# Feed-forward keys and gates for 512 tokens at once: wider matmuls behind a local-global attention kernel

## The chip, the cores and the metric

One core of one Trainium2 chip runs the whole program. The metric is device time in microseconds, the median of three runs: 692.88 us before the change (692.82 to 693.06).

## The reference, cut to what matters

```
for each of 8 batches, 8 heads of 64:          # attention
    global queries (32) attend to all 544 keys
    local queries (512) attend to 32 global keys and to local keys at most 32 away
x = heads side by side                          # 8 x (32 + 512) tokens x 512
xk = mu_k * x + (1 - mu_k) * x_prev             # token before, the first one sees zeros
xr = mu_r * x + (1 - mu_r) * x_prev
k = relu(xk @ w_k)                              # 512 -> 1024
out = sigmoid(xr @ w_r) * (k * k @ w_v)         # 1024 -> 512, gate of 512
```

All of it is asked for in float32. The weights arrive as float64 words.

## The kernel before

Everything is transposed: features lie on the 128 partitions and tokens along the free dimension, so a product for the feed-forward part is `weights (128x128, loaded into the array) x tokens (128x256, streamed)`. Each float32 operand is split into a high and a low part of the type fp32r, and a product is three matmuls: high by high, high by low, low by high (`products`, L506, the three at L508, L509 and L510).

For a batch there are two halves of 256 tokens (`Tokens`). For each half `mix` (L524) makes xk and xr as high and low parts (difference and weighted sum on DVE, high part by a cast on ACT, low part by a subtraction on POOL, L544). `squares` (L571) makes the keys: 8 blocks of 128 features, two to a PSUM bank, each of 4 x 3 matmuls; ACT takes the relu, DVE multiplies with the product. `gates` (L585) makes 4 blocks of the gate in the same way, with a tanh on ACT.

From batch 2 on (`FROM = 2`) the values `k*k @ w_v` go by seven products of half size instead of eight (`Keys`, L620). The four blocks B11, B12, B21, B22 of the squared keys (first or second half of the features, first or second half of the tokens) are combined to four others, T1 to T4 (`differences`, on DVE). Each block is split into high and low (`split`: cast on ACT, subtraction on DVE for B blocks and on POOL for T blocks), and multiplied with a combination of the value weights that is read back from DRAM (`load_left`, tiles `a`, five buffers, each product needs two). `values_1` makes three products of 24 matmuls each, `values_2` makes four; their results are added on DVE and ACT and multiplied with the gate in `write`, on POOL where the result lies in SBUF.

The attention of batch b+1 (`attention`, in pairs of units: scores, softmax on DVE, ACT and POOL, transposes on the PE, then `weighted`, the products with V) is recorded step by step between the steps of the feed-forward part of batch b (`beside_heads`). Its last result, `xT`, is what the next `mix` reads. The order in which the instructions really stand on each engine is set by a scheduler that works on this recording with its own idea of when an instruction becomes ready; `tc.high_priority()` moves an instruction ahead in it. Each engine then works strictly in that order. All DMAs stand in one queue, SP's.

In a batch of the steady state the PE's order is: `values_1` of the batch before, keys and gates of the first half, `values_2`, keys and gates of the second half, with the attention of the next batch in between. PSUM has three banks for the feed-forward part, four for scores and one for transposes.

## Time and profile before

| | us |
|---|---|
| median of 3 runs | 692.88 |
| lowest, highest | 692.82, 693.06 |
| span of the profiled execution, first to last instruction | 689.8 |
| between span and median | 3.1 |
| PE busy in the span | 663.3 (96%) |
| DVE, ACT, POOL busy | 425.9, 387.5, 359.4 |
| mean granted TensorE clock | 0.992 |

The profile is one execution on the same core, and 3.1 us of the time lie around its span. "Busy" of the PE counts a matmul from its start to a modelled end, some 280 ns for one of 128x256, though the next starts after a little over 110 ns; so what a matmul costs is read from the starts in the timeline or from the chain, not from the mean duration. Each matmul has a weight load of its own, shown as the engine PEld. Matmuls of plain float32 (attention) stand twice in the trace, since each is carried out in two passes.

### The profile page before, as it was taken

How to read it: one execution, taken by the hardware profiler on the slowest of the kernel's cores; microseconds unless marked ns; L12 is line 12 of the kernel's file. 1: busy time of each engine (PE TensorE's matmuls, PEld its weight loads, DVE VectorE, ACT ScalarE, POOL GpSimd, SP SyncE). 2: the span in 40 equal slices, each digit the busy share in tenths (PEclk: the TensorE clock that was granted, in tenths of full speed). 3: DMA queues.
4: the chain of work that ended last, by engine and by line, in shares of the span. 5: the costliest groups of instructions: out<-in, count | busy, mean ns of one | idle time of the engine just before them, and what ended most of it. 6: DMA issues, size and time to landing. Idle time of an engine off the chain costs nothing.

```text
span 689.8 us, 18729 instructions
## 1 busy us (share of the span) xinstructions
PE 663.3 (96%) x7530; PEld 626.6 (91%) x7530; DVE 425.9 (62%) x1221; ACT 387.5 (56%) x1058; POOL 359.4 (52%) x363
## 2 busy tenths in 40 slices
PE   6979999999998999999999999999999999999997
PEld 3769789989897999999999989999999999999997
DVE  5795977457557566545675657645575656377531
ACT  5876866366355565757457563747466644443530
POOL 5577595147777344565338244655348332642810
PEclk9989999999999999999999999999999999999999
DMA  8734353154737740544818092735727090535666
GB/s 343 299 122 169 124 196 127 48 185 141 254 131 253 248 157 29 210 159 151 310 67 302 12 358 92 263 105 204 256 97 271 2 334 34 200 119 172 207 197 208
DMA packets 43542, 123.37 MB, mean 179 GB/s; under 512 B 4032, under 2 KB 20928, under 8 KB 43456
## 3 DMA queue, kind: packets, MB, share of 16 engines
q1 hardware_dynamic: 43456, 122.18, 50.0%
q8 instruction: 59, 0.97, 0.5%
q14 instruction: 27, 0.22, 0.1%
HBM read 104.86 MB, written 17.30 MB: 177 GB/s over the span
## 4 chain that ended last, share of the span: by engine, by line
PE 67%; DVE 12%; POOL 7%; DMA 6%; issue 3%; ACT 3%; SPq 0%; POOLq 0%; ACTq 0%; DVEq 0%
PE ps_m L670 16%; PE ps_m L508 11%; PE ps_m L509 11%; PE ps_m L510 11%; PE ps_s L365 9%; DMA a<-scratch 4%; PE ps_t L394 3%; DVE xfull L539 2%; DVE Pt L333 2%; PE ps_t L361 2%; DVE diff L535 2%; PE ps_s L367 2%; DMA w<-w_k 1%; DVE B L651 1%; POOL Pt L349 1%
## 5 line engine op out<-in xcount | busy, mean ns | idle before, releaser
L508 PE MATMUL ps_m<-xkh,wk_h 128*128 128x256 f32 x544 | 154.3, 285 | 3.3 <-DVE xfull L539 3.3
L509 PE MATMUL ps_m<-xkl,wk_h 128*128 128x256 f32 x544 | 153.2, 282 | 1.0 <-POOL xkl L544 1.0
L510 PE MATMUL ps_m<-xkh,wk_l 128*128 128x256 f32 x544 | 152.5, 281 | 0.0
L670 PE MATMUL ps_m<-bh,a 128*128 128x256 f32 x736 | 137.5, 282 | 3.2 <-DMA a<-scratch 3.1
L339 ACT ACTIVATE Pt<-Pt,m 128x160 f32<-128x160 f32 x256 | 106.5, 419 | 26.7 <-DVE m L333 26.7
L670 PEld LDWEIGHTS ps_m<-bh,a 128*128 128x128 f32 x736 | 114.9, 188 | 6.1 <-DMA a<-scratch 3.7
L349 POOL TENSOR_TENSOR Pt<-Pt,ssum 128x512 f32<-128x512 f32 x64 | 67.4, 1053 | 80.7 <-DVE ssum L295 32.4
L508 PEld LDWEIGHTS ps_m<-xkh,wk_h 128*128 128x128 f32 x544 | 103.0, 190 | 4.9 <-ACT xkh L543 3.8
L509 PEld LDWEIGHTS ps_m<-xkl,wk_h 128*128 128x128 f32 x544 | 102.8, 189 | 2.5 <-POOL xkl L544 1.7
L510 PEld LDWEIGHTS ps_m<-xkh,wk_l 128*128 128x128 f32 x544 | 102.8, 189 | 0.0
L670 PE MATMUL ps_m<-bl,a 128*128 128x256 f32 x368 | 102.5, 279 | 0.0
L544 POOL TENSOR_TENSOR xkl<-xfull,xkh 128x512 fp32r<-128x512 f32 x34 | 46.8, 1375 | 85.9 <-ACT xkh L543 80.9
L582 DVE TENSOR_TENSOR B<-ps_m,relu 128x512 f32<-128x512 f32 x52 | 35.9, 690 | 72.1 <-ACT relu L580 72.0
L580 ACT ACTIVATE relu<-ps_m 128x512 f32<-128x512 f32 x52 | 31.0, 597 | 82.9 <-PE ps_m L510 80.7
L508 PE MATMUL ps_m<-xrh,wr_h 128*128 128x256 f32 x272 | 77.3, 284 | 0.0
L509 PE MATMUL ps_m<-xrl,wr_h 128*128 128x256 f32 x272 | 76.2, 280 | 0.0
L510 PE MATMUL ps_m<-xrh,wr_l 128*128 128x256 f32 x272 | 76.0, 279 | 0.0
L333 DVE CUSTOM_DVE_ANT_0 Pt<-ps_s,masks 128x160 f32<-128x160 f32 x256 | 65.9, 317 | 6.6 <-PE ps_s L365 4.9
L670 PEld LDWEIGHTS ps_m<-bl,a 128*128 128x128 f32 x368 | 69.2, 188 | 0.0
L617 POOL TENSOR_TENSOR gate<-sum,gate 128x512 f32<-128x512 f32 x18 | 26.8, 1489 | 59.7 <-DVE sum L716 39.9
L205 ACT CAST bh<-B 128x512 fp32r<-128x512 f32 x76 | 45.9, 620 | 18.0 <-PE ps_m L670 11.6
L508 PEld LDWEIGHTS ps_m<-xrh,wr_h 128*128 128x128 f32 x272 | 51.5, 189 | 1.2 <-ACT kkh L564 0.6
(146 smaller groups left out, 1594.6 us busy)
## 6 DMA issues: line engine op xcount, KB each, us to landing
a<-scratch SPq DMA_DIRECT2D x92, 512.0 KB, 5.9
raw_qk<-qk SPq DMA_DIRECT2D x32, 768.0 KB, 5.6
raw_v<-v SPq DMA_DIRECT2D x32, 640.0 KB, 6.0
out_l<-gate SPq DMA_DIRECT2D x32, 256.0 KB, 4.6
w<-w_k SPq DMA_DIRECT2D x8, 512.0 KB, 9.7
w<-w_v SPq DMA_DIRECT2D x8, 512.0 KB, 3.9
w<-w_r SPq DMA_DIRECT2D x4, 512.0 KB, 3.5
scratch<-wv_h SPq DMA_DIRECT2D x8, 256.0 KB, 2.8
```

Of the source, the lines that this page charges most:

```text
L205: nc.scalar.copy(hi, val)
L333: read = nc.vector.tensor_tensor_reduce(out=Pt[:, i], in0=place(e, t, h), in1=masks[:, e, slots[t][1]], op0=ALU.add, op1=ALU.min, scale=-s ...
L339: nc.scalar.activation(Pt[:, i], Pt[:, i], AF.Exp, bias=low_x[:, i:i + 1], scale=-1.0, accum_out=ssum[:, i:i + 1],)
L349: nc.gpsimd.tensor_mul(out, Pt[:, each, at:at + n], rinv.unsqueeze(2).to_broadcast([P, 4, n]))
L365: self.last = nc.tensor.matmul(*a, **kw)
L508: nc.tensor.matmul(out, w_h[:, i, cols], x_h(i), start=(i == 0), stop=False)
L509: nc.tensor.matmul(out, w_h[:, i, cols], x_l(i), start=False, stop=False)
L510: nc.tensor.matmul(out, w_l[:, i, cols], x_h(i), start=False, stop=(i == n - 1))
L544: nc.gpsimd.tensor_sub(lo[:, both], xf, hi[:, both].bitcast(F32))
L580: nc.scalar.activation(rk, kp, AF.Relu)
L582: nc.vector.tensor_mul(k2[f0 // HC][f0 % HC // 2], kp, rk)
L670: nc.tensor.matmul(out[:, j], w, x[:, i % 2], start=fresh and (i, j, n) == (0, 0, 0), stop=(i, n) == (HC - 1, 2), skip_group_check=True,)
```

## The change

From batch 2 on the keys and gates of a batch are made for all 512 tokens at once: a matmul streams 128x512 instead of 128x256, and there are half as many of them. A key block now fills a PSUM bank by itself. Only the first two batches and the global tokens stay at 256.

- `Batch.mix` makes xk or xr of 512 tokens, one feature block of 128 at a time. The two are made at different times now, since both use the same four buffers: xk before `values_1`, xr after the keys and before `values_2`.
- The order of a batch is now `values_1` of the batch before, all keys, `values_2`, all gates (`wide`). The first such batch (`first_wide`) has the gates ahead of the keys, and its xk in a pool of its own.
- The squared keys lie in tiles that hold both token halves, so that the blocks of the half-size products are strided parts of them (2 runs of 256). The number of half-size products, their matmuls (128x256), their weights and loads stay as they are. The split of T2 moves from the end of the batch into `values_1`, those of T3, T1, T4, B22 and of the next B11 and B21 follow one product each.
- The pools of the early part (`stage`, `mlp1`, `mlp`) are closed after batch 1, and new ones take their place (`ktp` 7 buffers, `partp` 5, as before `leftp` 5 and `sump` 3).
- The transposes of the attention get a priority of 400 in the scheduler, in all batches (`AHEAD`).

Two places show what that does to the order. First the PE, at the step from `values_1` to the keys in a batch of the steady state, before (`bh` and `bl` are the high and low parts of the blocks; `Pgl` and `Pt` belong to the attention):

```order
L394 MATMUL ps_t<-ident,Pt 128x128 x4
L367 MATMUL ps_s<-raw_qk 64x160
L365 MATMUL ps_s<-raw_qk 64x160 x15
L670 MATMUL ps_m<-bh,a 128x256
L670 MATMUL ps_m<-bl,a 128x256
L670 MATMUL ps_m<-bh,a 128x256 x2
L403 MATMUL ps_t<-ident,Pgl 128x128 x2
...
L508 MATMUL ps_m<-xkh,wk_h 128x256
L509 MATMUL ps_m<-xkl,wk_h 128x256
L510 MATMUL ps_m<-xkh,wk_l 128x256
```

and now, where the rows begin with the products with V (`PT`, `PG`, `PTg`) that make the last `xT` of the next batch:

```order
L371 MATMUL ps_s<-PG,raw_v 64x32 x20
L371 MATMUL ps_s<-PT,raw_v 64x64 x16
L371 MATMUL ps_s<-PTg,raw_v 128x2x64 x8
L401 MATMUL ps_t<-ident,Pt 128x128 x4
L659 MATMUL ps_m<-bl,a 128x256
...
L411 MATMUL ps_t<-ident,Pgl 128x128 x2
...
L373 MATMUL ps_s<-raw_qk 64x160
L371 MATMUL ps_s<-raw_qk 64x160 x15
L401 MATMUL ps_t<-ident,Pt 128x128 x4
L517 MATMUL ps_m<-xkh,wk_h 128x512
L518 MATMUL ps_m<-xkl,wk_h 128x512
L519 MATMUL ps_m<-xkh,wk_l 128x512
```

The matmuls of the keys are twice as wide. Between the products with V and the first key stood 69 of the 72 matmuls of `values_1` and 16 score matmuls; now it is 32 of them (27, two transposes, then 5), 16 score matmuls and 10 transposes.

Second POOL, in the same stretch. `xkl` is the low part of xk that the keys read; `gate<-sum` is the first result of `values_1` times the gate. Before, with `xkl` in halves of 128x512 for two feature blocks of 256 tokens:

```order
L544 TENSOR_TENSOR xkl_5397<-xfull_5403,xkh_5396 128x512 [waits PE_49,Activation_49,Pool_49]
...
L544 TENSOR_TENSOR xkl_5397<-xfull_5416,xkh_5396 128x512 [waits Activation_49]
L544 TENSOR_TENSOR xrl_5399<-xfull_5421,xrh_5398 128x512 [waits Activation_49]
L206 TENSOR_TENSOR bl_5577<-B12_5031,bh_5576 128x512 [waits PE_49,Activation_49]
L206 TENSOR_TENSOR bl_5581<-B12_5032,bh_5580 128x512 [waits Activation_49,Pool_49]
L206 TENSOR_TENSOR bl_5585<-B11_4449,bh_5584 128x512 [waits Activation_49]
L617 TENSOR_TENSOR gate_4591<-sum_5456,gate_4591 128x512 [waits DMAHW3_49,DMAHW5_49,DMAHW2_49,DVE_49]
```

and now, one `xkl` for each of four feature blocks of 512 tokens:

```order
L694 TENSOR_TENSOR xkl_6100<-xfull_6102,xkh_6099 128x512 [waits PE_49,Activation_49,Pool_49]
L694 TENSOR_TENSOR xkl_6100<-xfull_6108,xkh_6099 128x512 [waits Activation_49]
...
L212 TENSOR_TENSOR bl_6248<-kt_5300,bh_6247 128x512 [waits Activation_49]
L608 TENSOR_TENSOR gate_5982<-sum_6157,gate_5982 128x2x256 [waits DMAHW0_49,DMAHW1_49,DVE_49,Pool_49]
L212 TENSOR_TENSOR bl_6252<-kt_5351,bh_6251 128x512 [waits Activation_49]
L694 TENSOR_TENSOR xkl_6114<-xfull_6116,xkh_6113 128x512 [waits Activation_49]
L212 TENSOR_TENSOR bl_6684<-kt_5394,bh_6683 128x512 [waits PE_49,Activation_49]
L694 TENSOR_TENSOR xkl_6114<-xfull_6122,xkh_6113 128x512 [waits Activation_49]
```

The last two `xkl` stood ahead of the gate and of the splits of `values_2`; now they stand behind the gate and two splits.

The diff, cut to its core:

```diff
@@ transposes, transposes_of_g, transposes_global (the same in all three)
-            nc.tensor.transpose(tp[:, i], r.Pt[:, 4 * e + i, SG * e:SG * e + W], ident)
+            with tc.high_priority(AHEAD):
+                nc.tensor.transpose(tp[:, i], r.Pt[:, 4 * e + i, SG * e:SG * e + W], ident)
@@ class Batch(Values), new
+        def mix(self, of, pool=None):
+            mu = mu_k_sb if of == "k" else mu_r_sb
+            hs, ls = self.x[of] = [], []
+            for c in range(NC):
+                if c % 2 == 0:
+                    for part, x in ((hs, "h"), (ls, "l")):
+                        part.append((pool or mixp).tile([P, 2, SL], F32R, tag="mix", name=f"x{of}{x}"))
+                hi, lo = (part[c // 2][:, c % 2] for part in (hs, ls))
+                xT = xT_of(self.b, c)
+                diff, xf = (tmpp.tile([P, SL], F32, tag="tmp", name=name) for name in ("diff", "xfull"))
+                nc.vector.tensor_sub(diff, xT[:, 1:SL + 1], xT[:, 0:SL])
+                nc.vector.scalar_tensor_tensor(xf, diff, mu[:, c:c + 1], xT[:, 0:SL], op0=ALU.mult, op1=ALU.add)
+                nc.scalar.copy(hi, xf)
+                nc.gpsimd.tensor_sub(lo, xf, hi.bitcast(F32))
+        def keys(self):
+            for f in range(NF):
+                a, i = divmod(f, HC)
+                kt = self.blocks(a) if i % 2 == 0 else kt
+                kp = psum("m")
+                products(kp, wk_h, wk_l, slice(f * P, (f + 1) * P), *self.inputs("k"), NC)
+                square(kp, kt[:, i % 2].rearrange("p t n -> p (t n)"), lambda x: x)
+                yield
...
         def values_1(self):
...
+            self.split("T2")
             yield
...
-            t.write(0, c11)
+            self.write(0, 0, c11)
+            self.split("T3")
             yield
...
-            yield
-            self.split("T3", "T1", "T4")
+            self.split("T1")
+            yield
@@ the last level
+    def wide(this, before):
+        this.mix("k")
+        yield from before.values_1()
+        yield from this.keys()
+        this.mix("r")
+        yield from before.values_2(this.split)
+        this.differences()
+        yield from this.gates()
...
+    for b in range(FROM, B):
+        this = Batch(b)
+        steps = wide(this, last) if b > FROM else first_wide(this, last)
+        if b < B - 1:
+            beside_heads(steps, 19 if b > FROM else 16)
```

More of the change, by code (lines that the diff above doesn't have):

```diff
@@ L49 @@
 HUGE = 3.0e38
+AHEAD = 400
 REBIAS = 2.0 ** -112
@@ L705, in values_2 @@
             nc.scalar.copy(u3, X)
-            self.split("B22")
+            self.split("T4")
             yield
@@ L984, in local_global_attention_then_rwkv_ffn, with narrow_batch, first_wide @@
-    final = Keys([global_tokens()])
-    t, = final.tokens
-    for _ in batch(B - 1, last):
-        pass
-    last = keys_of[B - 1]
+    leftp = sump = ktp = partp = None
+    def narrow_batch(b, before):
+        sums = sums_of_values() if b == FROM - 1 else iter(())
+        for n, _ in enumerate(feed_forward(tokens_of(b), before)):
+            if n > FF_STEPS and n % 2:
+                next(sums, None)
+            yield
+        for _ in sums:
+            pass
+    def first_wide(this, before):
+        nonlocal leftp, sump, ktp, partp
+        this.mix("r")
+        yield from before.values()
+        valueu.close()
+        narrow.close()
+        ktp, leftp, sump = (place(*x) for x in (("ktp", 7), ("leftp", 5), ("sump", 3)))
+        mixed = ExitStack()
+        this.mix("k", mixed.enter_context(
+            tc.tile_pool(name="mixed", bufs=4, side="right", reuse_waits="tile")
+        ))
+        load_left()
+        load_left()
+        yield from this.gates()
+        yield from this.keys()
+        mixed.close()
+        partp = place("partp", 5)
+        this.split("B11", "B21")
+        this.differences()
@@ new lines, in wide, with place @@
+    def wide(this, before):
+        this.mix("k")
+        yield from before.values_1()
+        yield from this.keys()
+        this.mix("r")
+        yield from before.values_2(this.split)
+        this.differences()
+        yield from this.gates()
+    def place(name, bufs):
+        return last_pools.enter_context(tc.tile_pool(name=name, bufs=bufs, side="right", reuse_waits="tile"))
+    last_pools = ExitStack()
+    last = None
+    for b in range(1, FROM):
+        beside_heads(narrow_batch(b, last), 2 * FF_STEPS + 4)
+        last = feed_forward.last
@@ L990, in end @@
+    change_use(MIDDLE_USE)
+    for b in range(FROM, B):
[3 more added lines that the diff above has]
+            beside_heads(steps, 19 if b > FROM else 16)
+        else:
+            for _ in steps:
+                pass
+        last = this
+    t = global_tokens()
+    final = Globals(t)
     def end():
```

205 lines of the change are left out of this document (94 added, 111 removed).

## Prediction

> **What bounds the kernel now.** I read the engines' busy shares first, then the PE's waits, then the stretches of single batches, then the chain of waits.
>
> ```profile
> PE 663.3 (96%) x7530; PEld 626.6 (91%) x7530; DVE 425.9 (62%) x1221; ACT 387.5 (56%) x1058; POOL 359.4 (52%) x363
> PE ps_s L361 <- DMA raw_qk<-qk: 5.5, 2, 4.9
> PE ps_m L508 <- DVE xfull L539: 3.3, 1, 3.3
> PE ps_m L670 <- DMA a<-scratch: 3.1, 3, 1.5
> 270.00:347.00 77.00, 76.78 (x909) 73.35 (x908) 45.58 (x147) 44.79 (x128) 38.57 (x37) 1.00 0.50 186
> 347.00:424.00 77.00, 75.56 (x902) 72.47 (x901) 47.73 (x146) 44.70 (x127) 38.22 (x37) 1.00 0.51 186
> 501.00:578.00 77.00, 76.90 (x897) 74.36 (x896) 48.92 (x132) 43.27 (x115) 35.72 (x34) 1.00 0.46 165
> PE 67%; DVE 12%; POOL 7%; DMA 6%; issue 3%; ACT 3%; SPq 0%; POOLq 0%; ACTq 0%; DVEq 0%
> ```
>
> The PE is busy 96% of the span. The first two waits, for the first inputs and for the first mix, lie in the start that the change hardly touches. A batch of the steady state takes 77 us, and in the windows of 77 us the PE is busy for 75.6 to 76.9 of them (the number behind the window's length), at full granted clock (1.00). What idles there is mostly the wait for the value weights `a`, 3.1 us in all. So the bound is the pace at which the PE takes its matmuls, and a change pays only through fewer or cheaper ones. The 12% of DVE in the chain is no reserve: it followed releases back, while the PE had other work.
>
> **The wide matmuls.** From batch 2 on there are 6 batches, each with (32 + 16) blocks x 4 x 3 / 4 = 144 matmuls of 128x512 in place of 288 of 128x256: 8 key blocks and 4 gate blocks x 12, and twice that before. In all 864 pairs become one each. Their present price, from the chain and from starts in the PE's timeline:
>
> ```profile
> 611.33 5.44 PE ps_m L670 x48
> 413.31 0.28 PE L508 MATMUL ps_m<-xkh,wk_h 128*128 128x256 f32 x1
> 416.02 0.28 PE L510 MATMUL ps_m<-xkh,wk_l 128*128 128x256 f32 x1
> ```
>
> 48 matmuls in 5.44 us are 113.3 ns each. From 413.31 to 416.02 lie 23 steps of 2.71 us, 117.8 ns each: there are two paces, and in the stretches I looked at neither prevails. I take the middle, 115.5 ns, so 231 ns for a pair.
>
> What would one of 512 cost? No row of before shows one. What sets the pace of the narrow ones is seen in the attention:
>
> ```profile
> 434.73 0.22 PE L367 MATMUL ps_s<-PT,raw_v 128*64 128x64 f32 x1
> 435.66 1.31 PE L365 MATMUL ps_s<-PG,raw_v 128*64 128x32 f32 x40
> 436.80 1.13 PE L365 MATMUL ps_s<-PT,raw_v 128*64 128x64 f32 x32
> 419.55 0.60 PE L394 MATMUL ps_t<-ident,Pt 128*128 128x128 f32 x4
> L394 PE MATMUL ps_t<-ident,Pt 128*128 128x128 f32 x256 | 38.5, 275 | 2.8 <-POOL Pt L349 2.0 <-ACT xT L500 0.6 <-ACT PT L396 0.2
> L365 PE MATMUL ps_s<-raw_qk 128*64 128x384 f32 x36 | 7.6, 501 | 0.0
> L365 PE MATMUL ps_s<-raw_qk 128*64 128x32 f32 x36 | 2.3, 208 | 0.0
> ```
>
> With the last one's own 0.22 us taken off, the 40 of 32 columns start (1.31 - 0.22) / 39 = 28 ns apart and the 32 of 64 columns (1.13 - 0.22) / 31 = 29 ns: twice the columns, the same pace, with the same 64 columns of weights. The transposes load 128 columns of weights and stream 128: (0.60 - 0.275) / 3 = 108 ns. The matmul with 256 columns, with as large a load, takes 113. So up to here it is the load of the weights that sets the pace, and columns come nearly free. Long streams do cost: 384 columns against 32 cost 501 - 208 = 293 ns more, 0.83 ns for a column of plain float32. The fp32r ones stream 256 in at most 113 ns, 0.44 each, so they run at about double rate, 0.416; 512 columns are 213 ns, and some 3 ns for the change of matmul make 216, with the load hidden under the stream. A pair saves 231 - 216 = 15 ns, and 864 of them 13.0 us. That is the value I take. Bounds: no better per column than the fast pace, 226.6 ns, saves 3.8 us; the slow pace in all, 235.6 ns, costs 4.0 us; 213 ns saves 15.6 us.
>
> The Trainium skill (TensorE: Matmul & The Clock Gate, section "Back-to-back issue gap") gives N / 2.4 + 2.5 ns for a warm matmul; that would be 215.8 ns here, and the term 13.1 us. The same page (section "What overlaps and what doesn't" of the part on packing) says that a weight load overlaps a running matmul only where the row group differs, which would speak against hiding the load, since all these use the whole array; the pace of 113 ns for a load and a stream together speaks for overlap. It is a rival below.
>
> **Waits for `a`.** Two of the three lie in `values_2`, where the tile took long to land:
>
> ```profile
> 394.86 0.81 SPq L282 DMA_DIRECT2D raw_qk<-qk  x2
> 398.56 0.80 SPq L287 DMA_DIRECT2D raw_v<-v  x2
> 399.66 9.09 DMA a<-scratch
> 476.44 9.20 DMA a<-scratch
> a<-scratch SPq DMA_DIRECT2D x92, 512.0 KB, 5.9
> ```
>
> The median is 5.9 us; these two stood behind loads of qk and V issued just ahead (two of each, from 394.86 on, for the first). In the new order the products with V come at the very start of `values_2`, so V is loaded earlier and the later products of that stretch have 3 us or more of other work before a sixth tile is needed. I take 2.0 us as saved, of bounds 3.1 and -3 (as many waits again).
>
> **The mix of xk.** This is the step that gets worse. The mix for 512 tokens needs the last `xT`, and the queues of DVE and POOL hold other things between. Durations:
>
> ```profile
> L544 POOL TENSOR_TENSOR xkl<-xfull,xkh 128x512 fp32r<-128x512 f32 x34 | 46.8, 1375 | 85.9 <-ACT xkh L543 80.9 <-issue 5.0
> L206 POOL TENSOR_TENSOR bl<-B,bh 128x512 fp32r<-128x512 f32 x36 | 47.0, 1322 | 2.2 <-ACT bh L205 2.2
> L617 POOL TENSOR_TENSOR gate<-sum,gate 128x512 f32<-128x512 f32 x18 | 26.8, 1489 | 59.7 <-DVE sum L716 39.9 <-DVE sum L709 19.8
> L691 DVE TENSOR_TENSOR sum<-ps_m,sum 128x512 f32<-128x512 f32 x6 | 4.1, 686 | 4.7 <-PE ps_m L670 2.9 <-PE ps_t L394 1.8
> 437.86 1.16 PE L365 MATMUL ps_s<-PTg,raw_v 64*128 64x128 f32 x16
> 443.73 1.29 POOL L544 TENSOR_TENSOR xkl<-xfull,xkh 128x512 fp32r<-128x512 f32 x1 [1.02 <-ACT xkh L543]
> 449.51 0.28 PE L508 MATMUL ps_m<-xkh,wk_h 128*128 128x256 f32 x1
> 445.32 1.12 PE L365 MATMUL ps_s<-raw_qk 64*64 64x160 f32 x27
> ```
>
> Before, the products with V end at 439.0, the last `xkl` is done at 445.0, and the first key starts at 449.5: 4.5 us of slack. Now, with the end of the products with V as zero: the second product of `values_1` has 8 matmuls left, after four transposes, so it ends at about 0.6 + 0.9 + 0.2 = 1.7; DVE's sum 0.69; then POOL has the gate, a split, the third `xkl`, a split, the fourth `xkl`: 1.49 + 1.32 + 1.375 + 1.32 + 1.375 = 6.9. The fourth is there at 9.3. The PE has until then four transposes (0.6), 27 and 5 matmuls (3.6), two transposes (0.25), 16 scores (1.25) and four transposes (0.6), 6.3 us, and reads the fourth low part in the 11th matmul of the first key, 2.2 us later: at 8.5. So the PE waits about 0.7 us, where POOL runs at 1.3 us each 0.3 us; I take 0.5 in batches 3 to 6, 2 us. In the last batch there is no other attention: 36 matmuls of `values_1` follow the products with V (4.1 us), and the key needs the low part at about 6.1, while POOL's row is done at 9.1: 3 us. Together 5 us lost. Bounds: 0, where the operations overlap better, and 15 us, where POOL's share is 2 us longer in each of the five.
>
> xr has it easier: between the end of the keys and the gates lie at least 60 matmuls and the products with V, over 10 us for four `xkl`-like steps of 1.4. Its DVE work grows by the second difference only (as many elements as the first), with DVE at 62%.
>
> **The rest.** In the first wide batch the split of B11 waits for the keys' buffers, and only scores and two transposes lie ahead of its product: 1 us lost, bounds 0 and 3. The store of the gate in halves, the strided blocks and the splits in their new places cost the same instructions on engines at 52 to 62%; they are hidden behind the PE's 77 us, and where POOL's cover is gone it is counted above. The transposes ahead in the schedule are the same transposes; they change the first 255 us by chance, where the PE idles some 14 us, and I take 0, bounds 2 either way.
>
> **Sum**, against the profiled execution's own span: 689.8 - 13.0 - 2.0 + 5.0 + 1.0 = 680.8, and the 3.1 us between span and median give 683.9. I take the timed executions to have the same 3.1 us around a span. **Forecast: 684 us.**
>
> **Rivals.**
> 1. The wide matmul gains nothing per column over the fast pace (226.6 ns). For it: no fp32r of more than 256 columns is in the trace, and the rate of 0.416 is taken from plain float32. Against: the pace did not depend on columns where the load is the same. Time: 692.9 - 3.8 - 2.0 + 6.0 = 693.1, no change.
> 2. Slower: POOL's row in front of the fourth `xkl` becomes the new bound of a batch. One mechanism: where the normalisation of a scores unit stands there too, it adds 2 x (1.05 + 0.46) = 3.0 us:
>
> ```profile
> L349 POOL TENSOR_TENSOR Pt<-Pt,ssum 128x512 f32<-128x512 f32 x64 | 67.4, 1053 | 80.7 <-DVE ssum L295 32.4 <-ACT xrh L543 23.2 <-PE ps_s L365 10.7
> L349 POOL TENSOR_TENSOR Pgl<-Pt,ssum 128x128 f32<-128x128 f32 x64 | 29.7, 463 | 0.0
> ```
>
>    Then 5 x 3.0 more: 699 us. It decides once the waits exceed 14 us over five batches, 2.8 us each. Against it: in the order as it stands those normalisations come behind the fourth `xkl`, and POOL is half idle.
> 3. Better than the sum: POOL's row keeps pace, the waits for `a` go, and the start loses a little idle time: 692.9 - 13.0 - 3.1 + 1.0 = 677.8, with 1 us of the start 677.
> 4. The load is not hidden under a matmul of the same rows: 213 + 108 = 321 ns each, with the transposes' pace as the load's price, which by 864 x (321 - 231) is 78 us more: 692.9 + 78 - 2.0 + 6.0 = 775 us. The row of 113 ns for stream and load speaks against it. It is the rule of overlap of the Trainium skill (TensorE: Matmul & The Clock Gate) named above.
>
> That the change would not do what it says is excluded for the wide matmuls: the order shows them, 864 of them.
>
> **How the numbers follow.** Chances: the forecast's case 0.60 (679 to 689), rival 1 0.13, rival 2 0.10, rival 3 0.15, rival 4 0.02. About 0.2% (1.4 us) is what a measurement of this kernel can tell from no change. Faster: 0.60 + 0.15 and a third of rival 1, 0.79. Within 0.2%: a third of rival 1 and part of rival 2, 0.07. Slower: 0.14. The range, 677 to 691, takes in the forecast's case, most of rival 3 and the better side of rival 1, and leaves 0.2 out.
>
> **What would show it.** Starts of the wide matmuls 216 ns apart in the chain, and 864 of them: 227 or more would make rival 1 right. Waits of the PE on `xkl` of 0.5 us in a steady batch and 3 us in the last one; a batch of 77 us shortened to about 75. No wait for `a` over 1 us in `values_2`. The forecast is wrong if the PE idles over 10 us behind batch 2, or if the batch stays at 77 us while it does not idle.

## The result, and the profile after

The changed kernel takes 740.66 us (median of 4 runs, 738.59 to 741.18) against 692.85 us before (691.66 to 693.06, 4 runs on the same chip): a ratio of 1.069, with a 95% interval from 1.067 to 1.072. The forecast was 684 us, with a range up to 691. The profiled execution has a span of 738.6 us, 48.8 more than before.

The stages below are cut, in both traces, at the first half-size matmul of each `values_1`; the keys and gates of the first wide batch lie ahead of the first cut.

| stage | before, us | after, us | more |
|---|---|---|---|
| up to the first half-size product | 280.1 | 294.9 | 14.8 |
| batch stage 1 | 76.1 | 86.2 | 10.1 |
| batch stage 2 | 76.8 | 83.5 | 6.7 |
| batch stage 3 | 76.9 | 82.2 | 5.3 |
| batch stage 4 | 72.3 | 75.2 | 2.9 |
| batch stage 5 (attention runs out) | 56.2 | 63.5 | 7.3 |
| global tokens, and the end | 51.5 | 53.1 | 1.6 |

No stage became shorter. Busy shares, chain and the PE's waits after (in us: total, times, longest):

```profile
PE 688.3 (93%) x6666; PEld 598.6 (81%) x6666; DVE 463.4 (63%) x1173; ACT 387.9 (53%) x1058; POOL 380.5 (52%) x363
...
PE 51%; DVE 19%; POOL 12%; issue 7%; ACT 6%; DMA 4%; POOLq 0%; SPq 0%; DVEq 0%; ACTq 0%
PE ps_t L401 <- ACT PTg L412: 4.8, 3, 2.2
PE ps_m L659 <- ACT sum L756: 4.5, 3, 1.9
PE ps_t L411 <- DVE PT L403: 3.6, 4, 1.6
PE ps_t L401 <- POOL xrl L694: 3.1, 1, 3.1
PE ps_m L659 <- DMA a<-scratch: 0.7, 1, 0.7
```

The PE has 864 matmuls fewer and is busy 25 us longer. It now waits in many places for ACT, DVE and POOL, none of which is busy more than 63%. The windows of batch stages 1 to 3 show two things more (length of the stretch, then busy time of PE, PEld, DVE, ACT and POOL, then the granted clock):

```profile
294.90:381.10 86.20, 82.03 (x759) 68.38 (x759) 68.33 (x153) 46.32 (x132) 47.62 (x39) 0.96 0.50 166
381.10:464.60 83.50, 79.87 (x757) 68.58 (x755) 53.69 (x137) 46.93 (x132) 43.61 (x41) 0.96 0.50 171
464.60:546.80 82.20, 78.58 (x757) 67.30 (x755) 53.67 (x137) 44.25 (x126) 40.62 (x36) 0.98 0.51 174
```

DVE has 54 to 68 us of work in these stages, where it had 45 to 49 before, and the clock is no longer 1.00. One stall, from the timelines of PE, DVE and ACT in batch stage 2, shows how both come about:

```profile
434.49 1.60 DVE L692 SCALAR_TENSOR_TENSOR xfull<-diff,mu_k_sb,xT 128x512 f32<-128x512 f32 x1
436.20 1.60 DVE L691 TENSOR_TENSOR diff<-xT 128x512 f32<-128x512 f32 x1
437.71 0.69 DVE L755 TENSOR_TENSOR ps_m<-ps_m,sum 128x512 f32<-128x512 f32 x1
438.44 0.59 ACT L756 COPY sum<-ps_m 128x512 f32<-128x512 f32 x1 [3.55 <-DVE ps_m L755]
439.07 0.39 PE L659 MATMUL ps_m<-bh,a 128*128 128x256 f32 x1 [1.92 <-ACT sum L756]
439.30 0.28 PE L659 MATMUL ps_m<-bl,a 128*128 128x256 f32 x1
440.91 1.08 PE L401 MATMUL ps_t<-ident,Pt 128*128 128x128 f32 x4 [1.34 <-ACT PTg L412]
441.65 0.77 PE L659 MATMUL ps_m<-bh,a 128*128 128x256 f32 x2
442.22 0.41 PE L659 MATMUL ps_m<-bl,a 128*128 128x256 f32 x1
442.86 0.41 PE L659 MATMUL ps_m<-bl,a 128*128 128x256 f32 x1
```

The last matmul of product T3 starts at 431.7, but its sum (L755) stands on DVE behind the rest of both mixes, in the end behind two operations of the next batch's key mix of 1.60 us each. The PE waits 1.92 us for the copy behind that sum, then 1.34 us for the one PSUM bank of the transposes. From 442.22 to 442.86 lie three matmuls of 213 ns, where 120 is the pace a moment earlier: the clock is at half until 447. The same pair of waits ends at 522.5 and 524.4 us, with 3.4 us of half clock behind it. Summed over all distances from one start to the next (time at half clock included), the 48.8 us are 23.8 of pauses, 10.5 in the half-size products, 6.4 in the transposes, 3.6 in the attention, 1.2 in the values with the whole weights and 3.3 in keys and gates, where 13 less were forecast.

### The profile page after: what moved, and what is told of

Read it like the earlier page. It is cut to its first block, busy times and chain, and to the rows that moved or that the text cites. A ratio compares the mean times of both kernels' runs of the same rounds, so it can differ in the third digit from the quotient of the medians.

```text
span 738.6 us, 16955 instructions
## 1 busy us (share of the span) xinstructions
PE 688.3 (93%) x6666; PEld 598.6 (81%) x6666; DVE 463.4 (63%) x1173; ACT 387.9 (53%) x1058; POOL 380.5 (52%) x363
## 4 chain that ended last, share of the span: by engine, by line
PE 51%; DVE 19%; POOL 12%; issue 7%; ACT 6%; DMA 4%; POOLq 0%; SPq 0%; DVEq 0%; ACTq 0%
PE ps_m L518 10%; PE ps_m L517 10%; PE ps_m L519 10%; PE ps_m L659 9%; PE ps_s L371 5%; DVE xfull L692 4%; DVE diff L691 3%; ACT Pt L345 3%; PE ps_t L401 2%; DVE xfull L548 2%; POOL bl L212 2%; DVE bl L212 2%; PE ps_s L373 1%; POOL Pt L355 1%; DMA w<-w_r 1%
## 5 line engine op out<-in xcount | busy, mean ns | idle before, releaser
L518 PE MATMUL ps_m<-xkl,wk_h 128*128 128x512 f32 (+1 forms) x352 | 121.9, 347 | 2.6 <-POOL xkl L553 2.1
L517 PE MATMUL ps_m<-xkh,wk_h 128*128 128x512 f32 (+1 forms) x352 | 121.5, 351 | 1.7 <-DVE xfull L548 1.2
L519 PE MATMUL ps_m<-xkh,wk_l 128*128 128x512 f32 (+1 forms) x352 | 121.0, 344 | 0.0
L616 DVE TENSOR_TENSOR kt<-ps_m,relu 128x512 f32<-128x512 f32 x52 | 35.2, 689 | 72.5 <-ACT relu L614 72.2
L517 PEld LDWEIGHTS ps_m<-xkh,wk_h 128*128 128x128 f32 x352 | 66.2, 189 | 13.5 <-issue 3.3
L212 POOL TENSOR_TENSOR bl<-kt,bh 128x512 fp32r<-128x512 f32 x36 | 51.6, 1445 | 42.7 <-ACT bh L211 42.7
L517 PE MATMUL ps_m<-xrh,wr_h 128*128 128x512 f32 (+1 forms) x176 | 61.5, 351 | 3.3 <-DVE sum L769 1.8
L518 PE MATMUL ps_m<-xrl,wr_h 128*128 128x512 f32 (+1 forms) x176 | 60.6, 344 | 0.2 <-POOL xrl L694 0.2
L519 PE MATMUL ps_m<-xrh,wr_l 128*128 128x512 f32 (+1 forms) x176 | 60.5, 344 | 0.0
L694 POOL TENSOR_TENSOR xrl<-xfull,xrh 128x512 fp32r<-128x512 f32 x24 | 38.7, 1617 | 39.8 <-PE ps_s L371 25.7
L211 ACT CAST bh<-kt 128x512 fp32r<-128x512 f32 x76 | 46.1, 620 | 23.1 <-PE ps_m L659 22.9
```

Of the source, the lines that this page charges most:

```text
L211: nc.scalar.copy(hi, val)
L212: engine.tensor_sub(lo, val, hi.bitcast(F32))
L517: nc.tensor.matmul(out, w_h[:, i, cols], x_h(i), start=(i == 0), stop=False)
L518: nc.tensor.matmul(out, w_h[:, i, cols], x_l(i), start=False, stop=False)
L519: nc.tensor.matmul(out, w_l[:, i, cols], x_h(i), start=False, stop=(i == n - 1))
L616: nc.vector.tensor_mul(out, shape(kp), shape(rk))
```

## The experiments

The runs were made on several chips, on which the kernel before takes 690.6 to 692.9 us. So a difference of 2 us between two versions is within the scatter.

### What a wide matmul costs

A kernel of single prices, in place of the whole computation: groups of fp32r matmuls at several distances of their operands, groups behind pauses of the PE, subtractions on DVE with and without POOL.

> A kernel that computes nothing of the reference (it writes zeros, and a few sums, to the outputs) and only prices single things. 40 groups of 24 fp32r matmuls of 128x256, one behind the other, with the weights at 0, 64, 128, 192 or 320 bytes past a multiple of 512 and the streamed operand at 0 to 320 bytes past one; 9 groups of 128x512; then groups of 120 matmuls of 128x256 behind pauses of the PE of growing length (1, 2, 3, 4, 5, 7 copies on ACT in a chain, some 0.5 us each), and two pauses in a row with 12 matmuls between; then 6 subtractions of 128x512 on DVE alone and 6 beside 6 on POOL. Theory A (placement): in the traces the half-size products took 113 to 114 ns with weights 64 and the streamed part 0 bytes past a multiple of 512, and 120 ns with both at 64; so groups with both at one offset (modulo 128) should start 120 ns apart and the others 113 to 114. Rival B: the pace came from the other engines' work; then all groups show one pace. Width: 512 columns 226 to 236 ns, twice the pace of 256 (column-bound), in either; 216 ns if my prediction's price was right in a quiet chip. Pauses: theory C, a pause over about 2 us sets the granted clock to half for some 5 us (about 213 ns a matmul, 25 of them, 2.5 us lost), shorter ones don't; rival D, every pause over 1 us does it. DVE: 0.7 us alone, 1.3 to 1.6 us beside POOL.

The groups (start, length; W and X are the offsets of weights and streamed operand in bytes, N the columns):

```profile
42.44 2.89 PE L106 MATMUL W64X0N__382<-x,w 128*128 128x256 f32 x24
45.17 3.00 PE L106 MATMUL W64X32N__407<-x,w 128*128 128x256 f32 x24
48.00 3.04 PE L106 MATMUL W64X64N__432<-x,w 128*128 128x256 f32 x24
50.88 3.00 PE L106 MATMUL W64X96N__457<-x,w 128*128 128x256 f32 x24
...
149.63 5.76 PE L106 MATMUL W64X0N__1257<-x,w 128*128 128x512 f32 x24
155.23 5.62 PE L106 MATMUL W64X64N__1282<-x,w 128*128 128x512 f32 x24
160.69 5.67 PE L106 MATMUL W64X128N__1307<-x,w 128*128 128x512 f32 x24
```

From one start to the next, 24 matmuls of 256 columns take 2.73 us (113.8 ns each) with the weights 64 bytes further, and 2.88 us (120 ns) with both at the same offset. 512 columns take 5.60 us (233 ns) and 5.46 us (227.5), with nothing else on the chip. Two of 256 at the same offsets would be 227.6 and 240 ns: the wide one is 5 ns dearer in the first case and 12 ns cheaper in the second, and neither is 216. In the changed kernel the most frequent distance of the wide matmuls is that of the first case, 233 ns.

The second test does in the changed kernel what the wide matmul replaced. Each becomes two into the halves of the same bank:

```diff
-            nc.tensor.matmul(out, w_h[:, i, cols], x_h(i), start=(i == 0), stop=False)
...
+            for k, (w, x) in enumerate(((w_h, x_h), (w_h, x_l), (w_l, x_h))):
+                for at in range(0, wide, TOK):
+                    nc.tensor.matmul(out[:, at:at + TOK], w[:, i, cols], x(i)[:, at:at + TOK], ...)
```

> The changed kernel, each matmul of 128x512 done as two of 128x256 into the halves of the same bank, 1728 for 864, all else the same. If the wide matmul gains nothing (the pace is set by columns, 231 to 236 ns against 2 x 113 to 118): 737 to 744 us. If it gains the 15 ns a pair of the prediction and the gain is only eaten elsewhere: 753 us. If the weight load is what a wide matmul saves but clock and stalls hide it: between the two.

Measured: 739.68 us (739.31 to 741.07), the changed kernel's time within the measurement. The equal time alone doesn't settle it, since the scheduler also placed the attention otherwise: 1944 of its matmuls, not 1777, lie ahead of the first half-size product, and none, not 121, in batch stage 5, so that stages differ by up to 6 us in both directions. But the prices agree: in this trace the halves mostly start 113 to 118 ns apart, which is 226 to 236 ns for two, and the wide ones of the changed kernel mostly 231 to 236 ns. Width is worth nothing here. So the loss comes from what came with it.

### The priority of the transposes

The kernel before with `tc.high_priority(400)` around the three transposes (and nothing else), and the changed kernel without it.

> The kernel before, with only the priority of 400 on the transposes. Theory E: the priority puts transposes ahead of the work that feeds them, and it is this that made the idle time before the first wide batch grow (the half-size products start at 294.9 us after the change, at 280.1 before): 700 to 712 us, nearly all of the loss before 280 us. Rival F: the order of pools and the wider batches made it, and the priority alone costs nothing: 691 to 695 us.

> The changed kernel without the priority on the transposes. Theory E (the priority makes the loss at the start, and part of the stalls in the batches): 715 to 728 us. Rival F (it does not): 738 to 743 us. If transposes without priority come too late in the wide batches, which the priority was there for, above 745 us.

Measured: 703.59 us against 691.66 before (ratio 1.016, 1.013 to 1.019), and 732.48 us (1.059, 1.055 to 1.063), so the priority costs 12 us alone and 8 us within the change; the second lies between the ranges of theories E and F. In the first kernel the first half-size product starts at 290.5 us instead of 280.1. The PE's waits there:

```profile
PE ps_t L395 <- ACT PT L397: 3.7, 1, 3.7
PE ps_s L367 <- DVE m L333: 2.7, 4, 0.7
PE ps_t L395 <- ACT xT L503: 2.6, 1, 2.6
PE ps_t L395 <- POOL xkl L547: 2.0, 1, 2.0
```

L395 is the transpose. In the whole execution the PE idles 12.5 us in front of it, where it idled 2.8 in front of the same transposes before. It stands at the head of the PE's queue before its input or its bank is there: the wait of 3.7 us, up to 228.8 us, lies in the middle of a run of products with the whole value weights, which go on right behind the four transposes.

The wide batches might still want the priority: without it batch stage 5 takes 72.2 us, with it 63.5. So it was given only to the transposes of units behind the third batch (`AHEAD if attention.b > FROM else 0`).

> The changed kernel with the priority of 400 only for the transposes of units behind the third batch, so that the start is that of the kernel without the priority. Theory M (the priority costs 10 us ahead of the first half-size product and gains about 8 in the last wide batch: 63.5 us with it, 72.2 without): 728 to 732 us, first half-size product at 284 us, last wide batch at 64 to 66 us. Rival N (the last batch's gain comes from the whole schedule): 733 to 740 us.

Measured: 743.97 us (743.36 to 744.86), above the ranges of both theories. The first half-size product starts at 285.6 and batch stage 5 takes 63.4 us, as theory M had it, but batch stage 1 grows to 100.9 us (it takes in more of the attention, 524 of its matmuls instead of 392, and 9.4 us of pauses). What the order gains in one stage it gives back in another, and theory M's sum is refuted.

### The addresses

In the changed kernel the blocks `b` moved to the side of the memory where the value weights `a` lie, so that both stand at the same offset modulo 256 bytes (64); before they stood 64 bytes apart. The half-size products' most frequent distance went from 113 to 120 ns. In the test pads of 64 and 192 bytes between the pools set them 64 bytes apart again, with every instruction in its old order on all engines:

```diff
-    for side, n in (("left", 16), ("right", 104)):
+    for side, n in (("left", 16),):
...
+        apart(last_pools, "b", 16)
         partp = place("partp", 5)
```

> The changed kernel with the same instructions in the same order on every engine; only addresses move: gaps of 64 and 192 bytes between pools, so that value weights and the operand streamed past them lie 64 bytes apart (modulo 256) again, as before the change, and not at the same offset. Theory A (same offset costs 120 ns a matmul, 64 apart 114 to 118): the half-size products and the values of the first two batches fall from a mode of 120 to one of 113 to 118 ns; 1008 + 384 matmuls by 2 to 6 ns are 3 to 8 us: 732 to 738 us. Rival B (pace set by other things): 739 to 742 us, modes unchanged.

Measured: 738.53 us (1.068, 1.064 to 1.072), and the most frequent distances are 113 and 118 ns, no longer 120. The pace follows the addresses, as theory A has it, but in a kernel full of pauses most of it is not seen in the time. The clean test is the reverse, in the kernel before, where the PE hardly pauses (`("right", 104)` becomes 56, every instruction in its place):

> The kernel before, every instruction in its place; one pad of 104 floats is made 56, which puts the value weights at the same offset (modulo 256 bytes) as the operand streamed past them; before they were 64 bytes apart. Theory A: the values' matmuls go from a mode of 113 (mean 115 to 117 without waits) to 120; 1104 x 4.6 + 384 x 3 ns = 6.2 us: 696 to 699 us. Rival B: addresses cost nothing: 690.5 to 693 us.

Measured: 699.60 us against 690.57, ratio 1.012 (1.009 to 1.014), 9 us for 192 bytes, a little more than theory A expected. Timelines in the kernel before and in this one, where three matmuls lie from one `bl` to the next:

```profile
639.84 0.28 PE L670 MATMUL ps_m<-bl,a 128*128 128x256 f32 x1
640.18 0.28 PE L670 MATMUL ps_m<-bl,a 128*128 128x256 f32 x1
```

```profile
648.05 0.28 PE L670 MATMUL ps_m<-bl,a 128*128 128x256 f32 x1
648.41 0.28 PE L670 MATMUL ps_m<-bl,a 128*128 128x256 f32 x1
```

0.34 us before, 0.36 now. Over the whole traces the most frequent distance goes from 113 to 120 ns in the half-size products and in those with the whole value weights, which is some 7 of the 9 us (1104 x 5 and 384 x 4 ns). Most of the rest is in the keys and gates: their offsets stay, but they have 118 ns more often than 113. Then the key weights of the kernel before were moved from 320 to 64 bytes past a multiple of 512 (the tile `low` goes behind them), as the single prices suggested:

> The kernel before, the same instructions in the same order; the tile of the masks' lower part lies behind the key weights instead of ahead of them, which moves these by 768 bytes, from 320 to 64 bytes past a multiple of 512, with the streamed xk at 0. In the single prices 320 against 0 took 117.5 ns and 64 against 0 took 113.8. Theory A with that price: 1824 key matmuls, half of them at 117 to 118 now, gain 2 to 4 us: 687 to 689.5 us, faster than both kernels. Rival (the two paces of the keys have another cause): 690 to 692 us.

Measured: 691.85 against 691.97 us (1.000, 0.999 to 1.002). The keys keep both paces, 113 and 118. So the equal offset is shown to be dear for matmuls of 256 columns; what chooses between 113 and 118 is not shown.

### The stalls in the batches

First the stall shown above. The mix of the next keys is queued behind the sum on DVE:

```diff
+            Batch.sum_T3 = nc.vector.tensor_add(X, X, u2)
...
+                with tc.issue_after(Batch.sum_T3.ins) if late else nullcontext():
+                    nc.vector.tensor_sub(diff, xT[:, 1:SL + 1], xT[:, 0:SL])
```

> The changed kernel, with the mix of the next batch's keys held behind one sum of values_2 on DVE (order only, no wait for its end), from the third wide batch on. Theory G (the sum that the PE waits for stands behind two or three mix operations of 1.6 us on DVE, and the two pauses of 1.9 and 1.3 us that follow set the clock to half): the pauses of 1.9 and 1.3 us at the end of three or four batches and the 5 us of half clock behind them go, 5 us a batch: 722 to 730 us. Rival H (the pause only moves to the next thing that is late, the mix itself or PSUM of the transposes): 737 to 742 us.

Measured: 735.79 us (1.064, 1.058 to 1.069). Its four executions fall apart into 732.4 and 733.2, 738.4 and 738.7 us, and the profile is of the one with 738.4. Its windows of batch stages 2 and 3:

```profile
382.50:462.30 79.80, 77.27 (x757) 65.77 (x755) 53.61 (x137) 43.66 (x127) 40.45 (x38) 1.00 0.52 179
462.30:541.20 78.90, 77.20 (x757) 65.64 (x755) 53.09 (x135) 43.49 (x125) 41.27 (x37) 1.00 0.53 181
```

The pair of pauses is gone, the clock is back at 1.00, and the two stages are 3.7 and 3.3 us shorter. But stages 1, 4 and 5 became 1.6, 1.2 and 2.0 us longer (87.8, 76.4 and 65.5). That is theory G for the stall; the sum is between the ranges of G and H, and in the profiled execution it is H's.

Next, why DVE is late. The single prices have six subtractions of 128x512 alone (L152), and six with six on POOL beside them (L158; POOL's own in the third row); under them the mix of the changed kernel:

```profile
L152 DVE TENSOR_TENSOR o<-td,tb 128x512 f32<-128x512 f32 x6 | 4.1, 691 | 0.2
L158 DVE TENSOR_TENSOR o<-ta,tb 128x512 f32<-128x512 f32 x6 | 9.0, 1496 | 0.2
L159 POOL TENSOR_TENSOR o<-ta,tb 128x512 f32<-128x512 f32 x6 | 9.8, 1640 | 328.9 <-DVE ta L153 328.5
```

```profile
L691 DVE TENSOR_TENSOR diff<-xT 128x512 f32<-128x512 f32 x48 | 52.2, 1088 | 4.2 <-ACT xT L509 3.5
L692 DVE SCALAR_TENSOR_TENSOR xfull<-diff,mu_k_sb,xT 128x512 f32<-128x512 f32 x24 | 31.4, 1307 | 3.3 <-POOL xkl L694 1.9 <-POOL xrl L694 0.6
L692 DVE SCALAR_TENSOR_TENSOR xfull<-diff,mu_r_sb,xT 128x512 f32<-128x512 f32 x24 | 27.6, 1149 | 0.8
L769 DVE TENSOR_TENSOR sum<-ps_m,sum 128x512 f32<-128x512 f32 x6 | 4.1, 678 | 0.0
```

691 ns alone and 1496 beside POOL; in the kernel 1088 to 1307 on average, while a sum with one operand in PSUM keeps its price: 678 here, 686 to 690 before. Four kernels take work from the wide mix: the low parts subtracted on DVE instead of POOL; the low parts a mere copy on ACT (`nc.scalar.copy(lo, xf)`, so that the low part holds the whole value); no low parts at all, the high ones streamed twice; and no differences (`scalar_tensor_tensor(xf, xT[:, 1:SL + 1], mu, ...)`).

> The changed kernel with the low parts of the wide mixes subtracted on DVE instead of POOL (48 operations of 128x512; the scheduler moves some neighbours). Theory I (DVE's and POOL's operations of 128x512 float32 slow each other down, 0.69 us alone and 1.5 us together in the kernel of single prices): DVE's differences and weighted sums in the mix fall from a mean of 1.09 and 1.15 us to 0.7 to 0.8, the pauses at the sums shrink: 728 to 736 us. Rival J (DVE is simply too full; 48 x 0.7 us more on it make it later): 742 to 755 us.

> The changed kernel, in which POOL does no work in the wide mixes: their low parts are written by a plain copy on ACT (so xk and xr lose their split: the low part holds the whole value), the PE reads the same buffers as before. Theory I (DVE's SBUF operations of 128x512 stretch to 1.5 us beside POOL's, and the vector engines' burst behind the products with V is what the PE waits for): differences and weighted sums fall to 0.7 to 0.8 us on average, the pauses of 1.9 and 1.3 us go: 722 to 730 us. Rival J (the staging itself is too tight, whichever engine does it): 733 to 741 us.

> As the run before it, but the low parts of the wide mixes are left out altogether and the PE streams the high parts twice (the same number of matmuls; the result lacks the low parts). Two of the four buffers of the mix come free, so xr need not wait for xk. Theory I or the buffers: 715 to 728 us, batches of the steady state 77 to 79 us. Rival J: 733 us or more. The difference to the run before it is what buffers and ACT are worth.

> The changed kernel without the differences of the wide mixes (48 operations of 128x512 on DVE; the weighted sum takes the token itself in their place, so xk and xr are wrong by the token before). Theory I and the theory that DVE is too full both expect 724 to 732 us here; if it stays at 735 to 741 us, the PE's waits don't come from DVE's queue.

Measured, in that order: 735.55 us (1.063, 1.060 to 1.067), 718.66 (1.039, 1.036 to 1.042), 714.82 (1.034, 1.030 to 1.037), 715.68 (1.034, 1.031 to 1.037). Either POOL's part of the mix or DVE's differences, taken away, are worth 22 to 26 us, up to 8 us more than expected; on DVE in place of POOL only 5, at the slow end of theory I. The runs leave out more than the change added, since the kernel before has the same subtractions and half of the differences' columns. But there the PE pauses for only 3.3 us in the five batch stages together, so this can't explain 22 us. The mean of the differences fell less than expected with the copy on ACT:

```profile
L691 DVE TENSOR_TENSOR diff<-xT 128x512 f32<-128x512 f32 x48 | 44.8, 934 | 6.3 <-ACT xT L509 6.1
```

POOL's other work still lies beside them, which may be why; no run removed that too. Batch stages 2 and 3 of the kernel without differences:

```profile
375.50:451.90 76.40, 76.40 (x757) 65.64 (x755) 45.24 (x129) 43.59 (x124) 38.40 (x36) 1.00 0.54 187
451.90:528.20 76.30, 76.30 (x756) 65.55 (x754) 45.26 (x129) 44.84 (x128) 40.08 (x38) 1.00 0.54 187
```

The PE is busy without a gap, at full clock, and the stage takes 76.4 us. That is the kernel before's own batch (76.8), with DVE at 45 us, as it was then.

### The rest, and the parts together

The first wide batch, with two of its four gate blocks behind the keys, so that the PE has work while B11 is split:

> The changed kernel, where the first wide batch makes two of its four gate blocks behind the keys instead of all four ahead of them. Theory K (that batch is 10 us longer than before because the split of B11 waits for the buffers of the keys, and the PE has only scores and transposes meanwhile: pauses of 0.9, 0.65 and 1.1 us at its start and what follows from them): 734 to 738 us, the pauses on bh and bl gone. Rival L (the pauses go, but the mix of xk, which the gates covered, is late instead): 739 to 744 us.

Measured: 736.41 us (1.066, 1.063 to 1.068). The pauses on `bh` and `bl` are gone (0.9, 0.65 and 1.1 us); in their place stand 1.2 us for a copy of the transposes and 0.9 for `xkl`. So theory K holds for those pauses, but they are worth only 1.1 of the 10 us of the stage.

Repairs together: the priority off and the addresses apart; then all four repairs (addresses, order of the sum, late priority, split gates); then the first pair with the differences moved to ACT (`nc.scalar.activation(diff, xT[:, 0:SL], AF.Copy, scale=...)`), a whole kernel again; last the first pair without differences and low parts.

> The changed kernel without the priority on the transposes and with the addresses of the run with moved pools. If the two parts add: 732.5 minus what the addresses gave there (3 to 8 us), 725 to 729 us. If not, 730 to 735 us. Either way it stays over the kernel before, since what is left are the wide mix, the splits and the last two batches.

> The changed kernel with the repairs together: addresses 64 bytes apart, the key mix behind the sum on DVE, the priority only behind the third batch, the gates of the first wide batch split. If the parts add: 284 to the first half-size product, 82 for the first wide batch, 79 + 78 + 76 + 64 for the others and 52 for the end: 713 to 718 us. If each repair moves the wait to the next thing: 722 to 732 us. In no case under the kernel before, since the wide matmul itself gives nothing.

> A whole version of the wide kernel after these findings: no priority on the transposes, addresses 64 bytes apart, and the 48 differences of the wide mixes taken off DVE (ACT scales the token before by 1 - mu, DVE adds mu times the token; two tiles of 1 - mu more). From 730 us (priority and addresses mended), if DVE's burst is worth the 25 us that the run without differences gained: 705 to 712 us. If the burst's cost overlaps with what the priority cost: 712 to 722 us. Not under 692 us, as the wide matmul gives nothing.

> The wide kernel with everything out of its way, no whole computation: no priority, addresses 64 bytes apart, neither differences (xk and xr wrong by the token before) nor low parts in the wide mixes (the PE streams the high parts twice, the same number of matmuls). If the wide matmul is worth nothing, as the run with halves says, this is at best the time before plus what the start and the last batches keep: 690 to 702 us. If it is worth the 13 us of the prediction: 677 to 684 us.

Measured: 730.21 us (1.056, 1.054 to 1.059); 737.65 (1.068, 1.065 to 1.070); 731.69 (1.061, 1.056 to 1.066); 710.23 (1.027, 1.023 to 1.030). The first pair takes off 10.5 us, what the two gave singly (8.2 and 2.1). The four repairs do not add: they were expected at 732 us at most, and the late priority had been slower by itself. The last two are above their ranges too (722 and 702 us at most). Moving the differences to ACT gave nothing, 731.69 after 730.21, though leaving them out of the kernel with priority had given 25. Its batch stages 2 and 3 are 81.9 and 81.6 us long, with a new wait of 2.2 us for a copy on DVE in each; whether the priority or ACT's 34.6 us of new work makes that difference is open. The last kernel has batch stage 2 as follows:

```profile
359.20:436.60 77.40, 77.38 (x756) 65.47 (x755) 43.00 (x129) 44.32 (x127) 28.98 (x29) 1.00 0.53 185
```

With the differences and low parts out of the way, no pause and full clock, a wide batch takes 77.4 us, against 76.8 before. It starts its first half-size product at 279.8, as before the change, and its profiled execution still ends 21 us later than that of the kernel before (19 by the medians): 3 to 4 us each in batch stages 1 and 4, 9 where the attention has run out (68.6 + 32.0 against 56.2 + 35.3), 4 in the end. No version beat the kernel before.

## Why the prediction was wrong, step by step

**The bound** was read rightly (the PE's pace), and turned over: after the change the PE idles in every stage, for engines that are busy 52 to 63% over the whole. The result is 57 us over the forecast. Three steps failed: the gain of 13 for the width is not there, the mix, put at 5, costs some 20, and the priority, put at 0, costs 8 to 12.

**The wide matmuls, -13.0 us: wrong, nothing.** 233 ns instead of 216, and 739.68 us with halves. The step that failed is "up to here it is the load of the weights that sets the pace, and columns come nearly free". It set the transposes (128 columns, 108 ns) beside the fp32r products (256 columns, 113 ns) and took the equal price for that of the equal load. Its other evidence, 28 and 29 ns for 32 and 64 columns, comes from much shorter streams with half the weights, and no run tested what sets their pace. The transposes are plain float32: 128 x 0.83 = 106 ns, a price of columns; and 113 / 256 = 0.44 ns is one too, for fp32r. Then 512 columns are 226 to 236 ns. The rate of 0.416 was half of another type's rate and nothing measured. The 215.8 ns that the prediction has beside it from the Trainium skill (TensorE: Matmul & The Clock Gate, section "Back-to-back issue gap") differs from the measured 227.5 to 236 ns as well, and the measurement decides. The bounds (226.6 and 235.6) held; the value between them should have been their middle. Rival 1 was right on the matmul, and rival 4 is out: the weight load is hidden.

**Waits for `a`, -2.0: right in size.** They fell from 3.1 to 0.7 us. But with the PE slower than forecast, the loads had more time, so the reason given is not tested.

**The mix of xk, +5: right that it gets worse, wrong in place and size.** The first key of a batch waited for `xkl` of a wide mix 0.5 us once; POOL's row, worked out operation by operation, came in time. What came late was DVE, which I had put aside with "Its DVE work grows by the second difference only (as many elements as the first), with DVE at 62%". In a batch stage it makes 8 differences of 512 columns out of 8 of 256, each 1.09 us on average where one takes 0.69 alone, in the same stretch as POOL's subtractions that lengthen them. In batch stage 2 DVE's operations add up to 61.6 us instead of 55.8: the differences take 8.4 instead of 6.0, and most of the rest is in operations on as many elements as before that take longer. Removing both differences, or POOL's part, gave 22 to 26 us: that is nearer the size of the term than 5. Rival 2 named the mechanism for POOL, and priced it at 6 us over the kernel before.

The Trainium skill (SBUF — State Buffer, section "Who interferes with whom") says that a DVE instruction with two SBUF inputs contends with a GpSimd instruction that reads SBUF, and that one with at most one SBUF input, outside the two-port modes, does not. The rows agree: 691 against 1496 ns with two inputs in SBUF, and 678 for the sum with one of its inputs in PSUM. The rule spoke against the change and was not weighed in the prediction.

**Transposes with priority, 0 within 2: wrong, +8 to +12.** "I take 0, bounds 2 either way" was no estimate. The PE takes its instructions in the order of the program, so one that is moved ahead without being ready sooner holds up what is behind it; the waits of L395 above, 3.7, 2.6 and 2.0 us, are of this kind.

**The first wide batch, +1 of 0 to 3: the waits right, the stage not.** The splits cost 2.6 us of pauses, but the stage is 10.1 longer; DVE is busy for 68 of its 86 us. Without differences the stage is still 83.5 us, in the relieved kernel 79.4, so part of this stays open.

**"the strided blocks and the splits in their new places cost the same instructions": the same instructions, but dearer on the PE.** Their new addresses make a half-size matmul 120 ns; in the kernel before this is 9 us. In the changed kernel about 2 us of it show (740.66 to 738.53, and 732.48 to 730.21 without the priority), each time within the scatter.

**The clock.** No step of the prediction had it. A pause can cost twice, once as a pause and once as half clock behind it.

What is shown, then: priority 8 to 12 us, the vector work of the wide mixes 20 to 26, width 0, and for the addresses 9 us where nothing else waits; the 2 us in the changed kernel are not clear of the scatter. These are differences of whole kernels and overlap. What stays open is the last 19 us of the relieved kernel. The traces place nearly half of them where the attention runs out; in batch stage 2 the attention and its transposes take 22.0 us from start to start instead of 20.1. No run took this apart.

## What to carry to other kernels

A price per column must come from a matmul of the same type; two equal prices of unlike matmuls do not show a common cause. When work is gathered into larger pieces, look at the engines for the stretch in which it now falls and with the neighbours it will have there, not at shares of the whole span. A priority on an in-order engine helps only what is ready, and addresses belong to the change: compare the offsets of weights and streamed operand before and after.

## What the runs showed of the hardware

**Pauses and the clock.** Groups of 120 matmuls behind a pause of the PE (the pause in brackets):

```profile
257.06 13.89 PE L106 MATMUL bank<-xc,w 128*128 128x256 f32 x120 [2.26 <-ACT xc L130]
274.03 16.66 PE L106 MATMUL bank<-xc,w 128*128 128x256 f32 x120 [3.08 <-ACT xc L130]
```

After 2.26 us no matmul is slower; after 3.08 us some 26 take 213 to 214 ns, and the group takes 2.8 us more. In the changed kernel 1.92 and 1.34 us with two matmuls between them were followed by half clock too; in the prices 1.33 and 0.90 with twelve between them were not. The length alone doesn't decide it, though. A pause of 2.17 us was followed by half clock in the kernel before (from 211.5 us) and, in the run with the key weights moved, was not; in the changed kernel one of 1.81 us was (ending at 354.7), and one of 3.07 us was not (ending at 223.5). The stretches at half clock that end within a span are 3.4, 6.8 or 13.7 us long, and within a trace their starts are whole multiples of 3.41 us apart (47.7 and 211.5 us in the kernel before: 48 of them). So where a pause falls on this grid seems to count; no run moved one pause along it.

**Offsets.** Of the 40 groups the eight with equal offsets modulo 256 took 119 to 120 ns, four took 113.7 to 114.4 (64/0, 128/64, 192/128 and 0/192, weights first) and the others 117.4 to 119.6; among these, 0/96 and 192/32 were as dear as equal offsets. For 512 columns it is the other way round: 227.6 to 228.5 ns at equal offsets, 233 at 64/0. Behind the pauses, though, 64/0 ran at 114 in some groups and at 118 in others, so the offset is not the whole rule. The Trainium skill (TensorE: Matmul & The Clock Gate, section "Step-by-step: what each phase is for") says "Loading the next tile's weights doesn't steal SBUF read bandwidth from the running matmul." Here the pace depends on how the two operands lie to each other, by 5%, and the measurement decides.
